# Causal attention with a channel mix on one core: seven block products for the last two batches' product with w_v, 1/sum applied to the exponentials of pairs 13 to 24, and a new order

## The chip, the cores and the metric

The kernel runs on one core of one Trainium2 chip. The time is device microseconds (us) of one execution; the kernel before takes 459.02 us, the median of three runs (458.9 to 459.26). The engines are TensorE (PE, matmuls; PEld is its weight load), VectorE (DVE), ScalarE (ACT), GpSimd (POOL) and SyncE (SP, which issues the DMAs).

## The reference: what is computed

There are 4 batches, 12 heads of width 64 and 448 positions. The attention's result, 768 wide, goes into a channel mix:

```
scores = scale * q @ k.T, masked above the diagonal
attn   = exp(scores - max) / (sum + 1e-9)
x      = attn @ v, heads side by side             (448 x 768 per batch)
xk     = mu_k * x + (1 - mu_k) * x_prev           (xr likewise with mu_r)
k      = relu(xk @ w_k)                           (768 -> 1024)
out    = sigmoid(xr @ w_r) * ((k * k) @ w_v)      (1024 -> 768)
```

## The kernel before, in words

Two heads make a pair; pairs are numbered 0 to 23 in the code (pair 13 of the title is `w` = 12), six to a batch. For a pair, `score` (L388, L401) makes the scores in three pieces `s_w_0`, `s_w_1`, `s_w_2` in a ring of two PSUM tiles; `row_max` and `row_top` (L418, L430, L432) find the row maxima, `exps` (L441) writes the exponentials `e` and their row sums `su`. `prob_hi` and `prob_lo` (L495, L499) split `e` in a high and a low float16 part `p`, `turn_p` (L505, issued by SP) transposes it by DMA into `pT`, a ring of three buffers for two per pair, and `weighted_all` (L563) multiplies by v: 36 matmuls into the one PSUM tile `bank`, called PV w below. These are divided by the row sums on the way out: `recip`, `recip_hi`, `recip_lo` (L455, L459, L466) make 1/sum, `turn_r` (one PE transpose, L472), `copy_r`, `spread` (four matmuls of 128x112, L482) and `spread_out` (L492) lay it out over the partitions, and `evac` (L580) multiplies `bank` by it. `mix_now`, `mix`, `mix_hi`, `mix_lo` (L228 to L234 as `scaled`, L607, L614, L618) make xk and xr. Pairs 0 to 5 take other ways for some of this.

The products with w_k, w_r and w_v are `step_mm` (L830): an output block of 128 columns by 448 positions is summed in one PSUM tile of a ring of two, with three matmuls of 128x448 per 128 rows of the weight (high x high, high x low, low x high). In a batch mk has 8 outputs of 6 steps (144 matmuls), mr 6 of 6 (108), mv 6 of 8 (144). `relu` and `square` take mk out, `k_scale`, `k_hi`, `k_lo` scale and split it, `r_copy` and `sigmoids` (L937) take mr, `y_mul` (L941) multiplies mv by the sigmoid and `y_out` (L947) stores 128x448.

What sets the order is a table of numbers, not the loops: every operation has a number in `CHOICE["starts"]`, and `Plan.run` issues all operations sorted by it, so each engine's queue is that order cut down to its engine. `CHOICE["engines"]` names the engine for operations that may run on several, `CHOICE["fills"]` where matmuls that only fill time stand. Within the table each engine waits by semaphores for the last reader or writer of the tile that it touches. Batch b's mr and mv stand among the attention of batch b + 1; for the last batch they stand alone at the end.

Of the kernel before, what the change touches and what calls it, by code (L numbers as in the profile page):

```python
# [33 lines left out]
class Plan:  # L34
# [57 lines left out]
    "plain": "kr",  # L92
    "short": "LLLLLLRRRRRRRRRRRRRRRRRR",
# [7 lines left out]
def tile_causal_attention_channel_mix(  # L101
# [98 lines left out]
    def x_of(w):  # L200
        return x_ts[w % NX]

    N8 = 2 * NCH
    diag = [const.tile([P, 2], F32, name=f"diag{i}") for i in range(2)]
    for t in diag:
        nc.gpsimd.memset(t, 0.0)
    spreads = []

    rs_t = []
    for i in range(2):  # L210
        t = const.tile([CP, P], F16, name=f"rs{i}")
# [223 lines left out]
    def exps(w, g, j, c):  # L435
        if w not in tot:
            tot[w] = p2.tile([CP, NCH, 2], F32, tag="su", name=f"su_{w}")
        if (w, j) not in em:
            em[w, j] = act.tile([CP, NB, CP], F32, tag="e", name=f"e_{w}_{j}", bufs=NE)
        o = STEPS[g][c]  # L440
        nc.scalar.activation(  # L441
            em[w, j][:, blocks(c)].rearrange("p a b -> p (a b)"),
            sps[w, g][:CP, j, o : o + CP * (c + 1)],
            AF.Exp,
            bias=stat[w][:, c, j : j + 1],
            scale=scale,
            accum_out=tot[w][:, c, j : j + 1],
        )
# [92 lines left out]
    def weighted(w, n):  # L541
# [19 lines left out]
        for i, (vi, pi) in enumerate(steps):  # L561
            for j in range(2):
# [18 lines left out]

    def plain(b, kind):

        return b == 0 and kind in CHOICE["plain"]

    def as_one(t):

        return t.rearrange("p a s -> p (a s)").bitcast(F32)

    def share(w, mu, part):  # L590
        m = w % NPAIR
        if plain(w // NPAIR, "kr"[mu]):
            return (shares_p if whole_p(w) else shares_h)[:, part, mu, m : m + 1]
# [219 lines left out]
    def step_mm(m, kind, o, i):  # L813

        b, t0, n = M[m]
        steps, w = {"k": (NO, wk), "r": (NO, wr), "v": (NF, late.get("W"))}[kind]
        if i == 0:
            mps[m, kind, o] = ps_m.tile([P, 512], F32, tag="m", name=f"m{kind}_{m}_{o}")
        ps = mps[m, kind, o][:, :n]
        x = kk[b, i] if kind == "v" else {"k": xk, "r": xr}[kind][b * NPAIR + i]  # L820
        cols = slice(o * P, (o + 1) * P)
        if kind not in CHOICE["plain"]:
            w = w[:, i]
        else:
            half = w.shape[-1]
            h, lo = divmod(o * P, half)
            w = final(i + NO * (kind == "r"), h)
            cols = slice(lo, lo + P)
        for a, (wi, xi) in enumerate(((0, 0), (0, 1), (1, 0))):
            nc.tensor.matmul(  # L830
                ps,
                w[:, wi, cols],
                x[:, xi, t0 : t0 + n],
                start=(i == 0 and a == 0),
                stop=(i == steps - 1 and a == 2),
            )
# [57 lines left out]
    def k_scaled(m, pk):  # L894
# [468 lines left out]
```

## Time and profile before

| | |
|---|---|
| median of three runs | 459.02 us |
| the profiled execution | 458.52 us |
| its span | 456.7 us |
| PE / DVE / ACT / POOL busy | 450.7 / 352.8 / 298.2 / 180.0 us |
| PE's share of the chain that ended last | 87% |

The span is what the trace covers; 1.8 us of the execution lie around it. Busy time is the sum of an engine's instructions. A matmul's own time in the trace is longer than its share of a row of matmuls, since they overlap: the step from one to the next is read from a row's whole time and its count.

### The profile page before, as it was taken

To read this page: it belongs to the slowest core of one execution; us is meant where nothing else is said; L and a number is where in the kernel's file an instruction comes from. 1 tells how busy PE (TensorE), PEld (TensorE's weight loads), DVE (VectorE), ACT (ScalarE), POOL (GpSimd) and SP (SyncE) were. 2 spreads that over 40 slices of the span, in tenths; PEclk is the share of its full clock that TensorE was granted. 3 is DMA by queue.
4 is the path that set the end of the run, shared out by engine and by line. 5 is a ranking of instruction groups with operands and counts; after the bars stand their busy time and mean duration, and the time that the engine had idled before them with its cause. 6 is when DMAs were issued, how large, how long until landed. Compare 5 with 4: busy or idle time off the path is not lost.

```text
span 456.7 us, 9334 instructions
## 1 busy us (share of the span) xinstructions
PE 450.7 (99%) x3525; PEld 260.3 (57%) x3525; DVE 352.8 (77%) x711; ACT 298.2 (65%) x815; POOL 180.0 (39%) x179
## 2 busy tenths in 40 slices
PE   8999999999999999999999999999999999999996
PEld 6566765545655566555556566555656565555553
DVE  6999999998898999898898878777888685243111
ACT  5999999999989957676769545576459322322400
POOL 5255752132403651412466863247553652104000
PEclk9999999999999999999999999999999999999999
DMA  8897754674077686364478763741744672000011
GB/s 309 292 356 278 262 199 176 235 165 93 2 161 162 123 175 158 72 152 90 93 142 142 155 150 101 157 118 40 136 80 81 121 123 82 0 1 0 22 41 60
DMA packets 94845, 60.57 MB, mean 133 GB/s; under 512 B 83408, under 2 KB 86480, under 8 KB 94032
## 3 DMA queue, kind: packets, MB, share of 16 engines
q1 hardware_dynamic: 94800, 59.98, 51.7%
q8 instruction: 27, 0.44, 0.4%
q14 instruction: 18, 0.15, 0.1%
HBM read 33.82 MB, written 5.51 MB: 86 GB/s over the span
## 4 chain that ended last, share of the span: by engine, by line
PE 87%; ACT 6%; DVE 5%; issue 1%; POOL 0%; ACTq 0%; DVEq 0%
PE mv L830 22%; PE mk L830 18%; PE mr L830 14%; PE mk L845 8%; PE s L401 8%; PE bank L563 7%; PE mr L845 4%; ACT e L441 3%; PE s L388 2%; DVE s L418 2%; PE eT L521 2%; PE sp L482 1%; PE bank L284 1%; DVE p L499 1%; ACT turned L531 1%
## 5 line engine op out<-in xcount | busy, mean ns | idle before, releaser
L830 PE MATMUL mv<-k,wv 128*128 128x448 f16 x576 | 113.1, 353 | 0.0
L441 ACT ACTIVATE e<-s,st 112x112 f32<-112x112 f32 (+3 forms) x192 | 93.1, 495 | 12.6 <-DVE st L432 7.8
L830 PEld LDWEIGHTS <-wv 128*128 128x128 f16 x576 | 54.9, 98 | 50.7 <-issue 1.8
L830 PE MATMUL mk<-xk,wk 128*128 128x448 f16 x432 | 83.4, 353 | 0.0
L418 DVE TENSOR_REDUCE s<-s 112x2 f32<-112x672 f32 (+3 forms) x96 | 70.7, 743 | 15.0 <-PE s L401 11.3
L830 PEld LDWEIGHTS <-wk 128*128 128x128 f16 x486 | 46.5, 98 | 43.8 <-issue 2.2
L830 PE MATMUL mr<-xr,wr 128*128 128x448 f16 x270 | 55.3, 352 | 0.0
L499 POOL TENSOR_TENSOR p<-e,p 112x1120 f16<-112x1120 f32 x15 | 36.5, 2435 | 40.2 <-ACT p L495 31.1
L830 PEld LDWEIGHTS <-wr 128*128 128x128 f16 x270 | 26.1, 99 | 23.3 <-issue 0.2
L441 ACT ACTIVATION_READ_ACCUMULATOR e<-s,st 112x1 f32 x192 | 39.3, 205 | 0.0
L941 DVE SCALAR_TENSOR_TENSOR a<-mv,kap,a 128x448 f32<-128x448 f32 x24 | 16.3, 679 | 29.6 <-PE mv L830 29.4
L845 PE MATMUL mk<-xk,wk 128*128 128x448 f32 x96 | 38.0, 546 | 0.0
L607 DVE SCALAR_TENSOR_TENSOR xf<-xt,shares,xf 128x448 f32<-128x448 f32 x36 | 29.4, 823 | 1.4 <-ACT xf L228 0.8
L845 PE MATMUL mr<-xr,wr 128*128 128x448 f32 x72 | 29.8, 550 | 0.0
L563 PEld LDWEIGHTS <-vs 112*64 112x64 f16 x648 | 26.8, 110 | 4.9 <-issue 4.1
L563 PE MATMUL bank<-pT,vs 112*64 112x224 f16 (+1 forms) x648 | 29.4, 245 | 0.0
L499 DVE TENSOR_TENSOR p<-e,p 112x1120 f16<-112x1120 f32 x21 | 28.2, 1341 | 1.4 <-ACT p L495 1.3
L845 PEld LDWEIGHTS mk<-xk,wk 128*128 128x128 f32 x96 | 17.6, 190 | 16.4 <-issue 15.6
L495 ACT CAST p<-e 112x1120 f16<-112x1120 f32 x22 | 24.7, 1122 | 3.4 <-DMA pT<-p 3.2
L430 ACT ACTIVATE st<-s 112x2 f32<-112x2 f32 (+1 forms) x34 | 5.8, 169 | 32.3 <-DVE s L418 32.1
L614 POOL CAST xr<-xf 128x448 f16<-128x448 f32 x12 | 11.1, 924 | 39.1 <-DVE xf L607 39.1
L401 PE MATMUL s<-ql,qh 64*112 64x112 f32 (+3 forms) x144 | 25.5, 351 | 0.0
(216 smaller groups left out, 829.2 us busy)
## 6 DMA issues: line engine op xcount, KB each, us to landing
qk<-in_qk_dram SPq DMA_DIRECT2D x24, 448.0 KB, 4.3
wraw<-in_w_k_dram SPq DMA_DIRECT2D x6, 1024.0 KB, 7.9
wraw<-in_w_v_dram SPq DMA_DIRECT2D x8, 768.0 KB, 4.7
vraw<-in_v_dram SPq DMA_DIRECT2D x24, 224.0 KB, 5.0
out_dram<-a SPq DMA_DIRECT2D x24, 224.0 KB, 2.5
wraw<-in_w_r_dram SPq DMA_DIRECT2D x6, 768.0 KB, 5.5
pT<-p SPq DMA_TRANSPOSE x36, 4.8
muT<-in_mu_dram SPq DMA_DIRECT2D x1, 6.0 KB, 4.3
```

The source lines that it names most:

```text
L388: nc.tensor.matmul(diagonal, pick[rows, h], fill, start=h == 1, stop=False, skip_group_check=True)
L401: nc.tensor.matmul(s[:CP, j, o : o + n], q_[rows, 0, c * CP : (c + 1) * CP], k_[rows, 1, :n], start=False, stop=c == max(STEPS[g]) and i = ...
L418: nc.vector.tensor_reduce(most(w, g, c, c + 1), s[:CP, :, o : o + CP * (c + 1)], AX.X, ALU.max, negate=True)
L441: nc.scalar.activation(em[w, j][:, blocks(c)].rearrange("p a b -> p (a b)"), sps[w, g][:CP, j, o : o + CP * (c + 1)], AF.Exp, bias=stat[w] ...
L495: copy[e](p_t[at_][:, :NB, :CP], em[w, j])
L499: tt[e](p[:, NB:, :CP], em.pop((w, j)), p[:, :NB, :CP], ALU.subtract)
L563: nc.tensor.matmul(px[w][64 * j : 64 * j + 64, cols], value(j, vi), p(j, pi), start=n == 0 and i == 0, stop=last and i == len(steps) - 1, ...
L607: nc.vector.scalar_tensor_tensor(f, x_of(w)[:, :S], share(w, mu, 1), f, ALU.mult, ALU.add)
L614: copy[e](dst[w][:, 0], xf[w, mu])
L830: nc.tensor.matmul(ps, w[:, wi, cols], x[:, xi, t0 : t0 + n], start=(i == 0 and a == 0), stop=(i == steps - 1 and a == 2),)
L845: nc.tensor.matmul(mps[m, kind, o][:, :n], z[:, o * P : (o + 1) * P], x, start=i == 0, stop=i == NO - 1)
L941: nc.vector.scalar_tensor_tensor(s, mps.pop((m, "v", o))[:, : M[m][2]], kap[m][:, 3:4], s, ALU.mult, ALU.mult)
```

## The change

`"sums"` marks pairs 12 to 23 with N. For these `divide` scales the eight blocks of `e` in place on ACT by 1/sum (four activations a head, 112 x 112, 224, 336 and 448), before `prob_hi`; `recip_hi`, `recip_lo`, `turn_r`, `copy_r`, `spread` and `spread_out` are dropped, and `evac_up` multiplies `bank` by a constant on ACT or DVE.

`"fast": "v"` takes the products of batches 2 and 3 with w_v together: k*k of the two batches and w_v are cut in two by two blocks, and seven block products stand for eight. Two of them are plain `step_mm` groups of batch 2, five are `fast_mm`. `s_sum`, `s_hi`, `s_lo` make sums of weight blocks and split them, `t_sum`, `t_hi`, `t_lo` sums of k*k blocks; `keep` and `fold` add up the products from PSUM, `y_fast` multiplies by the sigmoid. The five products of output block p are summed in the two halves (`side` 0 and 1) of one PSUM tile `fast_p`. The last output is stored in two halves of 224 positions. `first_blocks` leaves only outputs 0 and 1 of batch 2's mv, four steps each and then four more, among batch 3's attention; the rest stands at the end. The `starts` and `engines` tables are new but for their first part.

```diff
+    "sums": "------HHHHHHNNNNNNNNNNNN",
+    "fast": "v",
...
+    def divide(w, j, e):
+        for c in range(NCH):
+            x = em[w, j][:, blocks(c)]
+            scaled(x, x, tot[w][:, c, j : j + 1], e)
+
...
+    def evac_up(w, e):
+        x, p = x_of(w)[:, 1:], px.pop(w)[:, :S]
+        if e == "A":
+            nc.scalar.activation(x, p, AF.Copy, scale=UP)
+        else:
+            nc.vector.tensor_scalar(x, p, UP, None, ALU.mult)
...
+    def t_sum(i, k, e="D"):
...
+            nc.vector.scalar_tensor_tensor(x, x, r1, b11[:, 0], ALU.mult, ALU.subtract)
+        elif k == 1:
+            tt[e](x, x, b11[:, 1], ALU.subtract)
...
+    def s_sum(i, k, e):
...
+            tt[e](sf[i, 0], w_block("21", i)[:, 0], w_block("21", i)[:, 1], ALU.add)
...
+    def fast_mm(p, q, i):
+
+        w, x, side, begins = {
+            3: ("s4", "b", 0, False), 4: ("22", "4", 1, False), 5: ("s1", "1", 0, True),
+            6: ("s2", "2", 1, True), 7: ("s3", "3", 1, False),
+        }[q]
+        if p not in ps_b:
+            ps_b[p] = ps_s.tile([P, 2, 512], F32, tag="s", name=f"fast_{p}")
...
+        for a, (wi, xi) in enumerate(((0, 0), (0, 1), (1, 0))):
+            nc.tensor.matmul(
+                ps_b[p][:, side, :S],
...
+    def fold(p, k):
+        side, was, to = {2: (1, 1, None), 3: (1, 1, None), 21: (1, 1, 1), 12: (0, 2, 2)}[k]
...
+        nc.vector.tensor_tensor(part_sum[p, to], ps_b[p][:, side, :S], part_sum[p, was], ALU.add)
...
+        if not early_sums(w):
...
+            if early_sums(w):
+                plan.op(
+                    {"ACT": 1690}, 0, divide, (w, j),
+                    [(te, None, "w"), (tu, None, "r")],
+                )
...
+            mm(5)
+            plan.op(copied(n, True), 0, keep, (p, 5, 0), [(bk, "b", "r"), (*m5, "w")])
+            mm(6)
+            plan.op("DVE", dve(n), fold, (p, 2), [(bk, "c", "r"), *[(*x, "r") for x in m1_], (*u2, "w")])
+            mm(7)
...
```

**First place: PE between two pieces of the scores of pair 23, and ACT beside it.** On PE before, a row `rp_22` and 24 matmuls of mv stand behind the last piece of `s_23_0` (the scores `s_23_1` come after PV 21, seven microseconds later by the trace):

```order
L401 MATMUL s_23_0_4771<-qh_23_4641 112x224 x2
...
L388 MATMUL s_23_1_4887<-mask_97,pick_96 128x48
...
L388 MATMUL s_23_2_4900<-mask_97,pick_96 128x48 [waits Activation_49]
```

On PE now, `s_23_1` follows `s_23_0` at once, then come 12 matmuls of mv, and then `s_23_2`, which takes the PSUM tile of `s_23_0`:

```order
L404 MATMUL s_23_0_4747<-qh_23_4674 112x224 x2
...
L391 MATMUL s_23_1_4765<-mask_97,pick_96 128x48 [waits Activation_49]
...
L404 MATMUL s_23_1_4765<-qh_23_4674 112x336 x2
...
L391 MATMUL s_23_2_4809<-mask_97,pick_96 128x48 [waits Activation_49]
```

ACT's queue now, at the exponentials of `s_23_0`; the wait of `s_23_2` on ACT is for the fourth of them:

```order
L1138 ACT_TABLE_LOAD
L1138 ACTIVATE a_162<-a_162,krs_2_4029 128x448 x4
L1138 ACTIVATE a_162<-a_162,krs_2_4029 128x448 [waits Activation_49]
L1138 ACTIVATE a_162<-a_162,krs_2_4029 128x448 [waits DVE_49]
L444 ACT_TABLE_LOAD [waits DVE_49]
L444 ACTIVATE e_23_0_4794,su_23_4793<-s_23_0_4747,st_23_4776 112x112 [waits PE_49]
L444 ACTIVATE e_23_1_4797,su_23_4793<-s_23_0_4747,st_23_4776 112x112
L444 ACTIVATE e_23_0_4794,su_23_4793<-s_23_0_4747,st_23_4776 112x224
L444 ACTIVATE e_23_1_4797,su_23_4793<-s_23_0_4747,st_23_4776 112x224
```

The room between the first and the third piece of pair 23's scores went from mv of half a batch to `s_23_1` and 12 matmuls.

**Second place: PE from PV 22 to PV 23, and SP.** On PE before, 48 matmuls of mv, a `rp` and two `sp` stand between the last matmul of PV 22 and the first of PV 23:

```order
L563 MATMUL bank_148<-pT_22_1_4979,vs_22_4929 64x112
L830 LDWEIGHTS wv_1099
L830 MATMUL mv_2_4_5024<-k2_2_0_4318,wv_1099 128x448 [waits DVE_49]
...
L482 MATMUL sp_23_5114<-rt_23_5112,sel_119 128x112 [waits Activation_49]
...
L563 MATMUL bank_148<-pT_23_0_5053,vs_23_4951 64x224 [waits DVE_49]
L563 LDWEIGHTS vs_23_4951
L563 MATMUL bank_148<-pT_23_1_5058,vs_23_4951 64x224 [waits DMAHW5_49]
```

On PE now, six matmuls of mk stand there:

```order
L576 MATMUL bank_148<-pT_22_1_4874,vs_22_4900 64x112
L852 LDWEIGHTS wk0_1779
L852 MATMUL mk_3_1_4980<-xk_18_4467,wk0_1779 128x448 [waits DVE_49]
...
L852 MATMUL mk_3_0_4892<-xk_21_4973,wk_150 128x448 [waits Activation_49]
...
L852 MATMUL mk_3_0_4892<-xk_21_4973,wk_150 128x448 [waits Pool_49]
...
L576 MATMUL bank_148<-pT_23_0_4922,vs_23_4966 64x224 [waits DVE_49]
...
L576 MATMUL bank_148<-pT_23_1_4970,vs_23_4966 64x224 [waits DMAHW4_49]
```

SP's queue now; the wait of the last transpose on PE is for the last matmul of PV 22, which reads `pT_22_0`, the buffer that `pT_23_1` takes (ring of three):

```order
L518 DMA_TRANSPOSE pT_22_0_4788<-p0_140 128x20x112 [waits DMAHW6_49,PE_49,Pool_49]
L518 DMA_TRANSPOSE pT_22_1_4874<-p1_142 128x20x112 [waits DMAHW7_49,DVE_49,PE_49]
L518 DMA_TRANSPOSE pT_23_0_4922<-p0_140 128x20x112 [waits DMAHW0_49,DVE_49,PE_49]
L518 DMA_TRANSPOSE pT_23_1_4970<-p1_142 128x20x112 [waits DMAHW1_49,DVE_49,PE_49]
L1149 DMA out_0_dram<-a_162 128x448 [waits DMAHW5_49,DVE_49]
```

Before, the same ring held and the same wait stood in SP's queue, but with mv behind it on PE.

**Third place: PE and DVE in the last tile, `fast_2`.** On PE before, the program ends with mv in two tiles in turn and no wait within a group:

```order
L830 MATMUL mv_3_4_5651<-k2_3_6_5459,wv_1099 128x448
L830 LDWEIGHTS wv_1099
L830 MATMUL mv_3_4_5651<-k2_3_7_5550,wv_1099 128x448
```

On PE now, `fast_2` stands alone for 60 matmuls; three matmuls after a block product is complete, a matmul waits for the DVE instruction that reads it, whichever half of the tile it writes itself:

```order
L1085 MATMUL fast_2_5670<-wk_150,sw_5_5400 128x448
L1085 LDWEIGHTS sw_0_5186
L1085 MATMUL fast_2_5670<-wk_150,sw_0_5186 128x448
...
L1085 LDWEIGHTS sw_1_5192
L1085 MATMUL fast_2_5670<-wk_150,sw_1_5192 128x448 [waits DVE_49]
```

DVE's queue now beside it (a wait on PE is for the matmul right ahead of the waiting one):

```order
L1114 TENSOR_TENSOR p0_140<-fast_2_5670,xt0_92 128x448 [waits DVE_49,PE_49]
L1114 TENSOR_TENSOR p1_142<-fast_1_5496,p1_142 128x448
...
L1114 TENSOR_TENSOR u3_2_5714<-fast_2_5670,xt0_92 128x448 [waits PE_49]
...
L1107 COPY p0_140<-fast_2_5670 128x448 [waits PE_49]
...
L1114 TENSOR_TENSOR xt0_92<-fast_2_5670,xt0_92 128x448 [waits PE_49]
...
L1143 SCALAR_TENSOR_TENSOR a_162<-mv_2_2_5459,kap_2_4013,a_162 128x224 [waits PE_49] x2
```

From the last products of `fast_0` to the end of the program there are six such pairs of a read and a matmul that waits for it: five reads of 448 positions and one of 224.

## Rows read from the trace of the kernel before

**Rows 1.** The page: busy time, and PE's granted clock in 40 slices.
```profile
PE 450.7 (99%) x3525; PEld 260.3 (57%) x3525; DVE 352.8 (77%) x711; ACT 298.2 (65%) x815; POOL 180.0 (39%) x179
PEclk9999999999999999999999999999999999999999
```

**Rows 2.** Chain that ended last, 366 us to the end: start, us, what.
```profile
368.35 0.20 PE sp L482 x4
...
373.09 0.05 PE rp L472
...
425.85 27.25 PE mv L830 x144
453.11 0.03 issue
453.13 0.68 DVE a L941
```

**Rows 3.** PE's waits: for what, us in total, times, longest.
```profile
PE bank L280 <- DVE busy L148: 1.1, 1, 1.1
PE s L388 <- ACT e L441: 0.6, 3, 0.2
```

**Rows 4.** Groups by form: busy us, mean ns of one, idle before.
```profile
L830 PE MATMUL mv<-k,wv 128*128 128x448 f16 x576 | 113.1, 353 | 0.0
L580 DVE TENSOR_TENSOR xt<-bank,xt 128x448 f32<-128x448 f32 x24 | 14.9, 620 | 3.8 <-PE bank L563 3.4
L607 DVE SCALAR_TENSOR_TENSOR xf<-xt,shares,xf 128x448 f32<-128x448 f32 x36 | 29.4, 823 | 1.4 <-ACT xf L228 0.8
L618 DVE TENSOR_TENSOR xk<-xf,xk 128x448 f16<-128x448 f32 x11 | 6.8, 616 | 2.0 <-ACT xk L614 1.3 <-POOL xk L614 0.7
L441 ACT ACTIVATE e<-s,st 112x448 f32<-112x448 f32 x48 | 30.1, 633 | 2.8 <-DVE st L432 2.3
L441 ACT ACTIVATE e<-s,st 112x112 f32<-112x112 f32 x48 | 16.8, 355 | 6.1 <-DVE st L432 5.3 <-DVE rs L466 0.3
```

**Rows 5.** The transposed `pT`: SP's instructions, then issue to landing.
```profile
L505 SPq DMA_TRANSPOSE pT<-p x36: 2553/2734/4880, 90.3 to 369.1; - x36
...
DMA to landing us min/median/max: 4.5/4.8/7.3
```

**Rows 6.** Timeline of PE at pair 23: start, duration, what.
```profile
354.80 0.25 PE L388 MATMUL s<-mask,pick 64*128 64x48 bf16 x4
...
355.40 0.25 PE L388 MATMUL s<-mask,pick 64*128 64x48 bf16 x4
...
364.90 1.64 PE L563 MATMUL bank<-pT,vs 112*64 112x224 f16 x36
...
376.10 1.64 PE L563 MATMUL bank<-pT,vs 112*64 112x224 f16 x36
```

**Rows 7.** Timelines of DVE and ACT at pair 23's first scores.
```profile
348.55 1.06 DVE L418 TENSOR_REDUCE s<-s 112x2 f32<-112x224 f32 x2
...
349.71 0.17 ACT L430 ACTIVATE st<-s 112x4 f32<-112x4 f32 x1 [0.21 <-DVE s L418]
349.95 1.28 ACT L441 ACT_TABLE_LOAD   x1
351.25 0.35 ACT L441 ACTIVATE e<-s,st 112x112 f32<-112x112 f32 x1
...
351.60 0.44 ACT L441 ACTIVATE e<-s,st 112x224 f32<-112x224 f32 x1
```

**Rows 8.** Stretches: us, then busy us of PE, PEld, DVE, ACT, POOL; clock.
```profile
40.00:60.00 20.00, 19.78 (x211) 14.04 (x211) 19.04 (x35) 19.23 (x57) 11.89 (x13) 1.00 0.71 237
60.00:80.00 20.00, 20.00 (x99) 10.63 (x94) 18.92 (x40) 19.56 (x49) 7.15 (x6) 1.00 0.60 215
...
160.00:360.00 200.00, 199.99 (x1724) 116.86 (x1719) 168.55 (x305) 130.04 (x374) 98.71 (x85) 1.00 0.57 121
...
360.00:456.70 96.70, 93.09 (x556) 49.42 (x553) 38.10 (x72) 21.44 (x46) 16.65 (x18) 1.00 0.18 45
```

More of the change, by code (lines that the diff above doesn't have):

```diff
@@ L834, in step_mm @@
                 start=(i == 0 and a == 0),
-                stop=(i == steps - 1 and a == 2),
+                stop=(i == steps - 1 or (kind == "v" and fast(m) and i == HK - 1)) and a == 2,
+                skip_group_check=kind == "v" and fast(m),
             )
@@ L907, in k_hi @@
         b, t0, n = M[m]
+        if (b, f) not in kk and fast(m) and m == B - 1:
+            kk[b, f] = x_home("b", f - NF // 2)
         if (b, f) not in kk:
@@ new lines, in s_home @@
+    def s_home(q, i):
+        if q == "3":
+            return w_block("21", i)
+        n = 3 * i + "124".index(q)
+        if n // 2 not in sw:
+            if n < 8:
+                t = act.tile([P, NB, CP], F32, tag="e", name=f"sw_{n // 2}", bufs=NE).rearrange(
+                    "p a b -> p (a b)"
+                ).bitcast(F16)
+            else:
+                t = act.tile([P, 2 * NB, CP], F16, tag="pT", name=f"sw_{n // 2}", bufs=NPT).rearrange(
+                    "p a b -> p (a b)"
+                )
+            sw[n // 2] = t[:, : 4 * HW].rearrange("p (n t c) -> p n t c", n=2, t=2)
+        return sw[n // 2][:, n % 2]
@@ new lines, in p_home, with keep @@
+    def p_home(p, n):
+        if n == 2:
+            return p2.tile([P, S], F32, tag=f"xf{p % 2}", name=f"u3_{p}", bufs=1)
+        z = p_all[(p_at[p]) % 2].rearrange("p a b -> p (a b)").bitcast(F32)
+        return z[:, n * S : (n + 1) * S]
+    def keep(p, k, slot, e):
+        if k == 1:
+            part_sum[p, 1] = a_slot(slot, S)
+            src = mps[B - 2, "v", p]
+        else:
+            part_sum[p, 5] = p_home(p, 0)
+            src = ps_b[p][:, 0]
+        copy[e](part_sum[p, k], src[:, :S])
@@ L1168, in values, with step @@
         over_all(lambda: vmm[b], 1, CP, f"v{b}", lambda r: scaled_v(b, r), out_, 600 if also else 525, also)
-    def step(m, kind, o, i):
+    def step(m, kind, o, i, part=None):
         b, t0, n = M[m]
-        if i == 0:
+        if i == 0 and not (part and part[0]):
             order[m, kind, o] = ("m", nexts("m"), 2)
@@ new lines, in tile_causal_attention_channel_mix, with s_tile, s_sums, sum_ @@
+    s_tiles = {}
+    def s_tile(q, i):
+        if q == "3":
+            return (f"w{2 * NO + i}", 0, 1), "21"
+        n = 3 * i + "124".index(q)
+        if n // 2 not in s_tiles:
+            s_tiles[n // 2] = ("e", 2 * NW + n // 2, NE) if n < 8 else ("pT", 2 * NW + n // 2 - 4 + S_FIRST, NPT)
+        return s_tiles[n // 2], n % 2
+    S_FIRST = 2
+    def s_sums():
+        n = HW
+        for i in range(HK):
+            w1, w2 = (f"w{2 * NO + i}", 0, 1), (f"w{2 * NO + HK + i}", 0, 1)
+            if i % 2:
+                f = [(("xf0", NW + i // 2, 1), None), (("xf1", NW + i // 2, 1), None), (("x", NW + NX - 1, NX), None)]
+            else:
+                t = ("pT", 2 * NW + i // 2, NPT)
+                f = [(t, 0), (t, 1), (("vs", NW + i // 2, NVS), None)]
+            def sum_(k, reads, at_):
+                plan.op(less(n, True), 0, s_sum, (i, k), [(x, p, "r") for x, p in reads] + [(*f[at_], "w")], fast=True)
+            def split(q, at_):
+                t, part = s_tile(q, i)
+                hi, lo = (part, part) if q == "3" else ((part, "hi"), (part, "lo"))
+                src = [(*f[at_], "r")]
+                plan.op(copied(n), 0, s_hi, (q, i), src + [(t, hi, "w")], fast=True)
+                plan.op(less(n, True), 0, s_lo, (q, i), src + ([] if q == "3" else [(t, hi, "r")]) + [(t, lo, "w")], fast=True)
+            sum_(0, [(w1, "21")], 0)
+            sum_(1, [(w2, "22"), f[0]], 1)
+            sum_(2, [(w2, "22")], 1)
+            sum_(3, [(w1, "11")], 2)
+            sum_(4, [f[2]], 0)
+            split("1", 1)
+            split("3", 0)
+            sum_(5, [f[1]], 2)
+            split("2", 2)
+            sum_(6, [(w2, "12"), f[2]], 1)
+            sum_(7, [(w2, "12")], 1)
+            split("4", 1)
@@ new lines, in tile_causal_attention_channel_mix, with first_blocks @@
+    p_at = {}
+    m1_of = {}
+    def first_blocks(m):
+        n = S
+        for p in range(HO - 1):
+            for i in range(NF):
+                ps = step(m, "v", p, i)
+                if i == HK - 1:
+                    at_, m1_of[p] = a_next(n)
+                    plan.op(copied(n, True), 0, keep, (p, 1, at_), [(ps, None, "r")] + [(x, None, "w") for x in m1_of[p]])
+            s = s_of[m, p]
+            plan.op("DVE", dve(n, ap=True), y_mul, (m, p), [(ps, None, "r")] + [(x, None, "w") for x in s])
+            plan.op("SP", 475, y_out, (m, p), [(x, None, "r") for x in s], dma=717)
@@ L1236, in mix_v @@
         for o in range(NO):
+            if m == len(M) - 1 and o == NO - 1:
+                for part in ((0, n // 2), (n // 2, n // 2)):
+                    for i in range(NF):
+                        ps = step(m, "v", o, i, part)
+                    s = [s_of[m, o][part[0] // HALF]]
+                    plan.op("DVE", dve(n // 2, ap=True), y_mul, (m, o, part), [(ps, part[0], "r")] + [(x, None, "w") for x in s])
+                    plan.op("SP", 475, y_out, (m, o, part), [(x, None, "r") for x in s], dma=360)
+                continue
             for i in range(NF):
```

298 lines of the change are left out of this document (258 added, 40 removed).

## The prediction

> **What bounds the kernel now.** I read the page first. PE is busy for 450.7 of 456.7 us, DVE for 352.8, ACT for 298.2, and PE's granted clock is full in every slice [rows 1]. So PE is the bound if nothing makes it wait, which the view of waits answers: in the whole span PE waits 1.1 us once, at the start, and 0.6 us in three short pieces [rows 3]. The chain of waits agrees: its last 85 us are rows of matmuls without a gap, then 0.03 us and one DVE multiplication of 0.68 [rows 2]. Hence every matmul taken out of that chain is worth its step, and every wait put into it costs its length. A row of 144 matmuls of 128x448 lasts 27.25 us [rows 2], so a step is 0.189 us. A single such matmul takes 0.353 [rows 4]: its result is complete 0.353 - 0.189 = 0.16 us after the next could have started.
>
> **PE's saving.** The change takes 228 matmuls of 448 positions out of step_mm, and adds 24 of 224 there (worth 12) and 180 in fast_mm: 36 steps fewer, 36 x 0.189 = 6.8 us. For 12 pairs the four spread matmuls (0.20) and the transpose of 1/sum (0.05) go [rows 2]: 12 x 0.25 = 3.0 us. Together -9.8 us. The last multiplication now covers 224 positions instead of 448, and its store half as much: I take -0.3 us, between 0 and half of 0.68.
>
> **First place: the wait of s_23_2, +1.3 us.** s_23_2 needs the PSUM tile of s_23_0, so it waits until the fourth exponential of s_23_0 is done. Before, half a batch of mv lay between. Now PE has only s_23_1 and 12 matmuls there: 0.60 us (one score's start to the next [rows 6]) + 12 x 0.189 = 2.9 us. Meanwhile DVE and ACT need, from the same work in the trace [rows 7]: two reductions 1.06, the row constant 0.17, ACT's table load 1.28, which stands behind that constant in ACT's queue because sigmoids came before, then four exponentials: 0.35 and 0.44 twice, overlapping by 0.1, about 1.4. With 0.05 at each of five hand-overs this is 4.2. The wait is 4.2 - 2.9 = 1.3; 0.6 if the hand-overs vanish and the exponentials overlap more, 2.5 if ACT comes late to it.
>
> **Second place: PV 22 to PV 23, +3.8 us, and +0.4 behind it.** The last transpose takes the buffer that PV 22 reads, and SP starts it when PV 22 ends. Its data land 4.5 to 7.3 us after issue, 4.8 in the median [rows 5]. PE's second matmul of PV 23 needs them. Before, 9.6 us of matmuls lay between the two (from 366.5 to 376.1 [rows 6]), so the landing was hidden. Now there are six steps, 1.1 us. With 0.1 for SP's start: 4.8 + 0.1 - 1.1 = 3.8 us, bounds 3.5 and 6.3 by the ends of the row. What stands behind the waiting matmul on PE is all of PV 23, and behind that the scaled and mixed x of pair 23: five instructions (taking the bank out, two for the mix, high and low part) of 0.62, 0.62 and 0.82 [rows 4] and two that I put between 0.36 and 0.62, about 2.7 together, against 12 matmuls, 2.3: +0.4. The other early-summed pairs keep over 5 us of matmuls between one PV and the next in the order, more than the landing.
>
> **Third place: the last tiles, +5.2 us.** In fast_p a fold or keep on DVE reads one half; the next matmul in PE's queue waits for that read, though it writes the other half, and the read itself waits for the matmul right ahead of it. Nothing lies between, so PE stands for the last matmul's completion (0.16), two hand-overs (0.03 [rows 2], and as much again) and the read. Before has no such read; the nearest row is the DVE instruction that takes the bank out of PSUM, 0.62 [rows 4]. That makes 0.16 + 0.06 + 0.62 = 0.84. Five of these are 4.2 us; the one of 224 positions I take at 0.65; one more a little earlier has three matmuls as cover, 0.84 - 0.57 = 0.3. Together 5.2. Below: 0.6 each if the completion is counted twice, 3.7 in all. Above: with the 0.82 of the mix row, 6.4. That these waits stop PE is sure by the order; nothing else may pass them in PE's queue.
>
> **What lies beside other work, at zero.** The 96 divisions go to ACT. They are nearest to exponentials of the same widths, 0.355 to 0.633 us [rows 4], mean 0.49: 47 us. From 160 to 360 us ACT is busy for 130 of 200 us and DVE for 169 [rows 8]; ACT with the divisions is near 177 of some 195. That PE can run full beside so loaded engines is shown earlier: from 60 to 80 us with ACT 19.6 and DVE 18.9 of 20 PE loses nothing, from 40 to 60 with 19.2 and 19.0 it loses 0.22 [rows 8]. So I take 0 and keep 2.2 (0.22 per 20 us) as its bound. The new DVE work (26 weight sums, 25 sums of k*k, 27 low parts, 12 folds, 9 products y_fast, each near 0.62 [rows 4], some 55 us, less 6 us of y_mul and some 12 of evac and spread_out) falls mostly after 360 us, where DVE is busy for 38 of 97 us [rows 8]. That hides it, except at the reads of the third place. If the cover were gone, each late low part would cost PE its 0.62.
>
> **The sum**, against the profiled execution of 458.52 us: 458.5 - 9.8 - 0.3 + 1.3 + 3.8 + 0.4 + 5.2 = 459.1 us. The profiled execution lies 0.1% under the median of 459.02, within what separates the runs; I predict 459.1. About 0.2%, 0.9 us, is what a measurement of this kernel can tell from no change.
>
> **Rivals.**
> - *The waits are mostly covered (faster).* If the trace of before holds here too, where no PE wait after the start is longer than 0.2 us [rows 3], only the sure savings and half of the waits stay: 458.5 - 10.1 + 5.4 = 453.8 us. For it: that order kept PE full beside two loaded engines. Against it: at the two last places no instruction on PE lies between, so cover would have to come from shorter landings and reads than any row shows.
> - *ACT becomes the bound in pairs 13 to 20 (slower).* One division chain per head stands between the exponentials and the split, so the score after next waits for the tile and PV for the transpose. It decides once ACT's work from one pair's first score to the next exceeds PE's. ACT at 177 of 195 leaves 1.5 us a pair; a pair that exceeds it by 0.3 us, 12 times, costs 3.6: 462.7 us. Against it are the two stretches above.
> - *The clock falls at the second place (slower).* Before, the clock is full in all slices, but PE never pauses longer than 1.1 us [rows 1, 3], so no row shows what a pause near 4 us does. If PE's clock fell to the lower of its two levels, 1.2 GHz, a step would take 0.378 us; for a stretch as long as the pause itself, 3.8 us, that loses 1.9, for twice as long 3.8: 461.0 to 462.9 us. The Trainium skill, page "TensorE: Matmul & The Clock Gate", section "HAM oscillation — how this bites in real kernels", says that waits of some microseconds for a DMA between rows of matmuls send the clock to half; by that rule this is the result, and nothing in the trace of before bears on it.
>
> **How the numbers follow.** My forecast has a chance of 0.50, its own range 457.3 to 461.3 us by the bounds of the terms (the lower ends take 0.7, 0.3 and 1.5 off, the upper ends together add more, but not all at once). The covered waits have 0.22, ACT 0.13, the clock 0.10; 0.05 is for what I do not see. The range that leaves two in ten out is 454.5 to 462.5 us. Faster than 458.1: the covered waits, 0.15 of the forecast and 0.01 of the rest, 0.38. Within: 0.25 of the forecast and 0.01, 0.26. Slower than 459.9: 0.10 of the forecast, ACT, the clock and 0.03, 0.36.
>
> **What the profile of the changed kernel would show.** The view of waits would have new rows of PE: for the transposed p, one of 3.5 to 4 us in front of PV 23; for ACT's exponentials, one near 1.3 us in front of a score; for DVE's folds and keep, five or six of 0.6 to 0.7 in the last 20 us. PE's busy time would be some 10 us less, and its clock full throughout. A granted clock under 1.00 after PV 23 would speak for the clock; ACT as releaser of PE between 160 and 300 us, in many pieces, for the second rival; a last stretch without waits for the first. The forecast is wrong if PE's new waits add up to less than 8 or more than 13 us, or if they lie elsewhere than at the three places.

## The result: 465.29 us, slower by 1.4%

The changed kernel takes 465.29 us in the median of four runs (464.78 to 465.64), the kernel before 458.96 beside it: a ratio of 1.0137, 95% interval 1.0123 to 1.0151. The profiled execution takes 464.78 us, its span is 463.0. The forecast was 459.1 with a range of 454.5 to 462.5, so the change is slower and the time lies outside the range.

The page of the kernel after, busy time and PE's granted clock, against [rows 1]:

```profile
PE 446.0 (96%) x3441; PEld 256.7 (55%) x3441; DVE 391.0 (84%) x797; ACT 352.0 (76%) x923; POOL 167.5 (36%) x161
PEclk9999999999999999999999999999999799999999
```

PE's busy time fell by 4.7 us and its idle time (span less busy) grew from 6.0 to 17.0, by 11.0: together +6.3, the difference of the spans. One slice, at 360 us, has lost clock. Where the idle time is, the timeline of PE after shows (start, duration, engine, line, operation, count; in brackets the wait ahead of it and what ended it):

```profile
54.92 0.31 PE L391 MATMUL s<-mask,pick 64*128 64x96 bf16 x4 [0.78 <-ACT turned L544]
...
155.75 0.25 PE L391 MATMUL s<-mask,pick 64*128 64x48 bf16 x4 [1.41 <-ACT e L444]
...
350.04 0.25 PE L391 MATMUL s<-mask,pick 64*128 64x48 bf16 x4 [1.39 <-ACT e L444]
...
359.68 1.60 PE L576 MATMUL bank<-pT,vs 112*64 112x224 f16 x35 [0.52 <-DMA pT<-p]
363.74 2.02 PE L852 MATMUL mk<-xk,wk 128*128 128x448 f16 x6 [2.46 <-DVE a L1143]
...
366.58 2.96 PE L576 MATMUL bank<-pT,vs 112*64 112x224 f16 x35 [0.49 <-DMA pT<-p]
369.47 4.88 PE L852 MATMUL mk<-xk,wk 128*128 128x448 f16 x21
...
439.50 2.44 PE L1085 MATMUL fast<-xt,wv 128*128 128x448 f16 x12 [0.72 <-DVE p L1114]
...
445.50 0.73 PE L1085 MATMUL fast<-wk,sw 128*128 128x448 f16 x3 [0.71 <-DVE p L1114]
...
449.78 0.73 PE L1085 MATMUL fast<-wk,sw 128*128 128x448 f16 x3 [0.71 <-DVE u L1114]
...
451.79 1.86 PE L1085 MATMUL fast<-xt,wv 128*128 128x448 f16 x9 [0.71 <-DVE p L1107]
...
455.50 1.30 PE L1085 MATMUL fast<-wk,sw 128*128 128x448 f16 x6 [0.71 <-DVE xt L1114]
...
458.78 1.02 PE L852 MATMUL mv<-k,wv 128*128 128x224 f16 x9 [0.54 <-DVE a L1143]
```

Before had none of these [rows 3]. By place: two waits in the first 160 us, 2.2; the first place (s_23_2) 1.39; the second (PV 22 to PV 23) 0.52 + 2.46 + 0.49, and 0.17 at 374.51, 3.6; the last tiles 0.72 + 4 x 0.71 + 0.54, 4.1. That is 11.3, near the 11.0 of idle time that came.

At the second place the clock is the other half. Stretches of the kernel after (us, busy us of PE, PEld, DVE, ACT, POOL, PE's granted clock, DMA share, GB/s):

```profile
362.00:364.00 2.00, 0.26 (x2) 0.16 (x2) 2.00 (x4) 1.13 (x2) 0.89 (x1) 1.00 0.56 103
364.00:366.00 2.00, 2.00 (x7) 0.56 (x6) 2.00 (x6) 0.67 (x1) 0.15 (x1) 0.54 1.12 214
366.00:368.00 2.00, 1.51 (x21) 1.42 (x21) 1.40 (x4) 0.00 (x0) 0.00 (x0) 0.50 0.62 222
...
370.00:372.00 2.00, 2.00 (x10) 0.90 (x8) 1.74 (x4) 0.58 (x2) 0.00 (x0) 0.75 0.01 4
```

After the wait of 2.46 us PE runs at 0.50, the lower of its two levels (1.2 GHz), until about 371 us. The Trainium skill, page "TensorE: Matmul & The Clock Gate", section "HAM oscillation — how this bites in real kernels", says that waits of some microseconds for a DMA between short rows of matmuls send the clock to half. The trace agrees on the half clock, with the 0.50 above; but the longest wait here is 2.46 us, for an instruction of DVE, while the page's case has longer ones.

### The profile page after: what moved, and what is told of

Its sections match the earlier page's. It is cut to its first block, busy times and chain, and to the rows that moved or that the text cites. A ratio compares the mean times of both kernels' runs of the same rounds, so it can differ in the third digit from the quotient of the medians.

```text
span 463.0 us, 9335 instructions
## 1 busy us (share of the span) xinstructions
PE 446.0 (96%) x3441; PEld 256.7 (55%) x3441; DVE 391.0 (84%) x797; ACT 352.0 (76%) x923; POOL 167.5 (36%) x161
## 4 chain that ended last, share of the span: by engine, by line
PE 76%; DVE 11%; ACT 6%; DMA 4%; issue 2%; POOL 1%; ACTq 0%; DVEq 0%; SPq 0%
PE mk L852 17%; PE mr L852 13%; PE mv L852 10%; PE mk L868 8%; PE fast L1085 7%; PE s L404 7%; PE bank L576 6%; PE mr L868 3%; DVE s L421 3%; ACT e L444 3%; DMA pT<-p 2%; PE s L391 2%; DMA wraw<-in_w_r_dram 2%; DVE p L512 1%; DVE wk L762 1%
## 5 line engine op out<-in xcount | busy, mean ns | idle before, releaser
L444 ACT ACTIVATE e<-s,st 112x336 f32<-112x336 f32 (+3 forms) x192 | 92.8, 492 | 13.2 <-DVE st L435 7.2
L852 PE MATMUL mv<-k,wv 128*128 128x448 f16 (+1 forms) x372 | 71.9, 347 | 0.6 <-DVE a L1143 0.5
L512 POOL TENSOR_TENSOR p<-e,p 112x1120 f16<-112x1120 f32 x17 | 40.5, 2383 | 44.5 <-DVE p L508 22.3
L852 PEld LDWEIGHTS <-wv 128*128 128x128 f16 x372 | 35.1, 98 | 32.5 <-issue 3.4
L231 ACT ACTIVATE e<-e,su 112x112 f32<-112x112 f32 (+1 forms) x96 | 42.2, 516 | 2.7 <-DVE su L463 2.7
L627 DVE SCALAR_TENSOR_TENSOR xf<-xt,shares,xf 128x448 f32<-128x448 f32 x36 | 26.5, 739 | 1.8 <-ACT xf L231 1.3
L512 DVE TENSOR_TENSOR p<-e,p 112x1120 f16<-112x1120 f32 x19 | 25.2, 1328 | 1.3 <-ACT p L508 1.1
L728 POOL TENSOR_SCALAR wraw<-wraw 128x768 int32<-128x768 uint16 (+1 forms) x17 | 19.4, 1142 | 17.0 <-DMA wraw<-in_w_v_dram 9.1
L1085 PE MATMUL fast<-wk,sw 128*128 128x448 f16 x108 | 21.9, 352 | 2.3 <-DVE p L1114 0.7
L391 PE MATMUL s<-mask,pick 64*128 64x48 bf16 (+3 forms) x288 | 19.7, 213 | 4.4 <-ACT e L444 3.3
```

What stands on the lines that cost most here:

```text
L231: nc.scalar.activation(dst, src, AF.Copy, scale=s)
L391: nc.tensor.matmul(diagonal, pick[rows, h], fill, start=h == 1, stop=False, skip_group_check=True)
L444: nc.scalar.activation(em[w, j][:, blocks(c)].rearrange("p a b -> p (a b)"), sps[w, g][:CP, j, o : o + CP * (c + 1)], AF.Exp, bias=stat[w] ...
L627: nc.vector.scalar_tensor_tensor(f, x_of(w)[:, :S], share(w, mu, 1), f, ALU.mult, ALU.add)
L728: nc.gpsimd.tensor_scalar(t, u, TOP3, -0.499, ALU.mult, ALU.add)
L852: nc.tensor.matmul(ps, w[:, wi, cols], x[:, xi, t0 : t0 + n], start=(i == 0 and a == 0), stop=(i == steps - 1 or (kind == "v" and fast(m) ...
```

## What holds PE up at the second place

The chain of waits of the kernel after from PV 21 to the work behind PV 23 (start, us, what):

```profile
353.44 6.20 DMA pT<-p
...
359.73 0.76 DVE p L508
...
360.51 1.34 DVE p L512
...
361.91 4.63 DMA pT<-p
...
366.58 2.96 PE bank L576 x32
```

Two landings stand in a row, not one. Pair 23's second split (L508, L512) writes the p buffer that the transpose of pair 22 still reads. It begins when that has landed, 6.20 us after its issue, and only then can the last transpose go, 4.63 more. Behind the split in DVE's queue stands y_mul (L1143), which frees the PSUM tile that the six matmuls of mk take: that is PE's 2.46. So the end of this place is set by landing, split, landing; how the wait divides among PE's instructions matters little. How much the first landing adds can be read too. DVE's timeline has a wait of 0.90 us for it ahead of the split, but the last transpose also waits for the last matmul of PV 22, which ends at 361.28 (359.68 + 1.60), and it went at 361.91. Without the first landing it could have gone some 0.6 us earlier at most, an estimate from these rows.

## The experiments

Diffs leave out the table of numbers and the places of the fills, which are renumbered. Each run of a kernel was compared with the kernel before on the same chip.

**Keep PE busy around PV 23 (e1_fill).**

```diff
+    def warm(w, n):
+        t = ps_t.tile([P, 512], F32, tag="t", name=f"warm_{w}")
+        for i in range(n):
+            nc.tensor.matmul(t[:, :P], busy, busy, start=i == 0, stop=i == n - 1, skip_group_check=True)
...
+        if w == NW - 1:
+            warm(w, 28)
         for n in range(len(PV)):
             weighted(w, n)
+        if w == NW - 2:
+            warm(w, 40)
```

> 68 matmuls of 128x128 without use, into the small PSUM tile that nobody reads, keep PE busy in the two long waits between PV 22 and PV 23 (40 right behind PV 22, 28 right ahead of PV 23); nothing else is moved. After has PE's clock at 0.50 to 0.54 from 364 to 370 us. Theory: the clock falls because PE stands still there; with the filler it stays at 1.00, the waits keep their ends, and the time falls by what the low clock cost: six mk matmuls 0.9, PV 23 1.4, 21 mk matmuls 0.9, together 3.2 us, less up to 0.5 that the filler is longer than the waits: 462.1 to 462.6 us. Rival: the rows are slow there for another reason (transfers that run beside them); then the clock column stays low and the time is 465.3 to 465.8.

Measured: 464.02 us (463.15 to 465.54), ratio to before 1.0095 [1.0062, 1.0128]. PE's timeline:

```profile
360.33 1.60 PE L576 MATMUL bank<-pT,vs 112*64 112x224 f16 x35 [0.52 <-DMA pT<-p]
361.87 2.41 PE L588 MATMUL warm<-busy 128*128 128x128 f16 x40
364.39 1.29 PE L861 MATMUL mk<-xk,wk 128*128 128x448 f16 x6
...
367.18 1.68 PE L576 MATMUL bank<-pT,vs 112*64 112x224 f16 x36
...
371.79 1.67 PE L861 MATMUL mk<-xk,wk 128*128 128x448 f16 x8 [0.31 <-DVE xk L647]
```

The clock stays at 1.00, PV 23 takes 1.68 instead of 2.96, the six matmuls of mk 1.29 instead of 2.02. Yet from PV 22's wait to the row of mk that follows km (374.51 after, 373.63 here) it is 13.30 us instead of 14.83: 1.5 gained. The six matmuls lay inside the landing's wait anyway, and an x that the slow clock had hidden is now waited for, 0.31. By the profiles the clock costs 1.5 net, half of the 3.2 expected; its gross price is worked out further down, with PE's saving. The medians differ by 1.3, and the intervals of the two ratios overlap (1.0062 to 1.0128 here, 1.0123 to 1.0151 after); e10_three shows the gain clear of the noise.

**Half 0 of fast_2 in a tile of its own (e2_bank).**

```diff
+        to = bank if p == HO - 1 and side == 0 else ps_b[p][:, side]
...
-                ps_b[p][:, side, :S],
+                to[:, :S],
...
-        nc.vector.tensor_tensor(part_sum[p, to], ps_b[p][:, side, :S], part_sum[p, was], ALU.add)
+        src = bank if p == HO - 1 and side == 0 else ps_b[p][:, side]
+        nc.vector.tensor_tensor(part_sum[p, to], src[:, :S], part_sum[p, was], ALU.add)
```

> Half 0 of the last tile fast_2 is put into the PSUM tile bank, which is free by then; the same matmuls and DVE instructions in the same order. Theory: PE's waits in the tail stand between halves of one tile that share no data; with two tiles four of the waits of 0.71 us (0.85 with the last matmul's completion) go, and two reads keep three matmuls as cover (0.28 each): 465.3 - 3.4 + 0.6 = 462.5 us. Rival: DVE, with folds and y_fast, sets the pace of the tail; then the waits move to the next fold and the time stays within 0.5 us of 465.3.

Measured: 460.18 us (458.54 to 461.86), ratio 1.0018 [0.9999, 1.0038]. PE's timeline at PV 23 and in the last tile:

```profile
366.71 1.94 PE L576 MATMUL bank<-pT,vs 112*64 112x224 f16 x35 [0.16 <-DMA pT<-p]
...
449.77 2.43 PE L1086 MATMUL bank<-wk,sw 128*128 128x448 f16 x12
452.04 1.60 PE L852 MATMUL mv<-k,wv 128*128 128x224 f16 x15
454.18 1.02 PE L852 MATMUL mv<-k,wv 128*128 128x224 f16 x9 [0.54 <-DVE a L1145]
```

The four waits of 0.71 are gone. From the row of mk that follows km to PE's last matmul it is 81.8 us (373.42 to 455.20) instead of 85.3 (374.51 to 459.80): 3.5 us, which is 4 x (0.71 + 0.16), so the completion of the last matmul is lost with each wait, as the forecast had it; the 0.28 expected to stay at each of two reads did not. The rest of the 5.1 is mostly the second place, where in this profile PV 23 took 1.94 us and not 2.96, since the clock came back sooner. That differs between executions of this kernel: the six with a granted clock of 0.996 in the mean of the span take 458.54 to 460.21 us, the four with 0.992 or 0.993 take 460.65 to 461.86. All four of the changed kernel have 0.993. At like clock the tile is worth its 3.5 and little more: 465.3 less the 461.5 that those four take in the median is 3.8.

**y_mul ahead of the split (e3_ymul):** `y_mul(2,1)` moved in DVE's queue before `prob_hi(23,1)`.

> Only y_mul of batch 2's output 1 is moved, on DVE, from behind the split of pair 23's second head to ahead of it, so that the PSUM tile for mk's output 1 is free when PV 22 ends; the wait of 2.46 us on PE that the trace puts down to it goes. Theory A (landing): the last transpose's landing ends the stretch, and PE now waits in front of PV 23 for the 2.5 us longer: 465.3, within 0.6 us. Theory B (DVE's queue): the 2.46 us were the cost, and the time falls to 462.8.

Measured: 465.9 us (465.18 to 467.45), ratio 1.0137 [1.0104, 1.0169]. PE's timeline:

```profile
365.34 0.35 PE L852 MATMUL mk<-xk,wk 128*128 128x448 f16 x1 [1.12 <-ACT xk L634]
366.45 0.54 PE L852 MATMUL mk<-xk,wk 128*128 128x448 f16 x2 [0.77 <-POOL xk L638]
...
368.78 2.96 PE L576 MATMUL bank<-pT,vs 112*64 112x224 f16 x35 [1.57 <-DMA pT<-p]
```
```profile
368.00:370.00 2.00, 1.22 (x17) 1.22 (x18) 1.53 (x5) 0.00 (x0) 0.00 (x0) 0.50 0.70 243
```

The wait for y_mul is gone and 1.12 + 0.77 + 1.57 = 3.46 stand in place of 2.46 + 0.49 = 2.95: the landing sets the end, whichever matmul waits. The second fence is the stretch in which PV 23 begins, its clock behind the five busy times: it fell here too (0.50), though no wait is longer than 1.57 us. This profile is of the longest of the four executions, 467.45 us with a mean clock of 0.989; the others, at 0.993, take 465.18 to 465.91, as the changed kernel does.

**The order of before up to pair 9's scores (e4_first).** Only the table of numbers changes. The cut lies near 122 us by the trace, not at 185 as I had put it.

> The operations up to the first score of pair 9 (some 185 us) stand in the order of the kernel before; everything from there on is that of the changed kernel. Theory: the new order of the first part brought PE's waits of 0.78 us (at 54.9) and 1.41 us (at 155.8); they go, and since PE is the bound from there on, nothing later gives the time back: 465.3 - 2.2 = 463.1 us, without these two rows of waits. Rival: a later chain (sigmoids, exponentials, transposes at pair 23) sets the end whatever happened before it, or the first part's waits come from the new operations and not its order: 465.3, within 0.5 us.

Measured: 465.28 us (464.48 to 468.48), ratio 1.0132 [1.0088, 1.0176]. The wait at 55 us is gone, that at 155 us stays, 1.42, since the cut is ahead of it. PE's rows from PV 23 on, in the profiled execution of 464.48 us:

```profile
365.83 2.96 PE L576 MATMUL bank<-pT,vs 112*64 112x224 f16 x35 [1.31 <-DMA pT<-p]
368.72 5.30 PE L852 MATMUL mk<-xk,wk 128*128 128x448 f16 x21
374.19 4.13 PE L852 MATMUL mk<-xk,wk 128*128 128x448 f16 x21 [0.17 <-DVE km L911]
```

The landing moved with PE: PV 23's second matmul starts 0.75 us earlier than after (366.58), and its wait is longer mainly because the six matmuls of mk ran at full clock (1.29 us instead of 2.02). The slow clock takes back over half of it: it ends near 371 us in both profiles, so the row of 21 mk lasts 5.30 instead of 4.88, the row behind km starts 0.32 us earlier and the span is 0.3 shorter. The median did not change, against the expectation.

**The same up to pair 12's scores (e8_first).**

> The changed kernel, with the order of before up to the first score of pair 12, so that both waits that the new order brings in the first 160 us (0.78 at 55 us, 1.41 at 156 us) should go. Theory (these waits are an addition of their own): 465.3 - 2.2 = 463.1 us. Rival (what PE gains early is given back at PV 23, where it waits for a transposed p whose time is set by DVE, ACT and SP): the waits in front of PV 23 grow by as much, and the time stays at 465.3.

Measured: 478.0 us (473.72 to 478.84), ratio 1.0395 [1.0347, 1.0444]. It tells nothing of the first part: the seam between the two orders brings worse waits of its own. Rows of DVE, then the one of PE that waits for it:

```profile
152.33 1.33 DVE L512 TENSOR_TENSOR p<-e,p 112x1120 f16<-112x1120 f32 x1 [4.97 <-ACT p L508]
...
154.56 0.62 DVE L593 TENSOR_TENSOR xt<-bank,xt 128x448 f32<-128x448 f32 x1
```
```profile
155.23 3.01 PE L576 MATMUL bank<-pT,vs 112*64 112x224 f16 x36 [5.50 <-DVE xt L593]
```

DVE's instruction that takes out the bank stands behind a low half whose high half ACT makes late, behind a batch's sigmoids. Inconclusive.

**The table load in ACT's idle time (e5_exp).**

```diff
             nc.scalar.activation(sg[m, o], sg[m, o], AF.Sigmoid, scale=krs[m])
+        if m < B - 1:
+            nc.scalar.activation(first_in, first_in, AF.Exp)
```

> The changed kernel with one exponential of a single element on ACT right behind the sigmoids of batches 0 to 2, so that ACT's table load (1.28 us) stands in its idle time before the first row maxima and not between the row constant and the exponentials. Theory (the load is on the path to s_23_2 and s_10_2): the wait at s_23_2 goes from 1.39 to about 0.5 us, that at s_10_2 from 1.41 to about 0.4, and the chain to PV 23 comes 0.8 earlier: the time falls by 1.7 to 2.6 us, to 462.7 to 463.6. Rival (the exponentials' wait is for the reductions, and the load is beside them): both waits stay and the time stays at 465.3.

Measured: 462.02 us (461.76 to 462.82), ratio 1.0064 [1.0047, 1.0081]. Rows of PE, then of ACT:

```profile
154.37 0.25 PE L391 MATMUL s<-mask,pick 64*128 64x48 bf16 x4 [0.41 <-ACT e L444]
347.93 0.25 PE L391 MATMUL s<-mask,pick 64*128 64x48 bf16 x4 [0.65 <-ACT e L444]
```
```profile
344.86 1.28 ACT L1140 ACT_TABLE_LOAD   x1
346.15 0.20 ACT L1140 ACTIVATE firstin<-firstin 128x1 f32<-128x1 f32 x1
```

The load now lies between the sigmoids and the row constants; the wait at s_10_2 fell from 1.41 to 0.41, that at s_23_2 from 1.39 to 0.65. The medians differ by 3.3 us, the two profiled executions by 2.0; the two waits explain 1.7. The profiled execution has the mean clock of the kernel after, 0.993, and the other three have 0.996, so 2.0 is the gain at like clock.

**Only the divisions, in the order of before (e6_sums).** `"sums"` with N for pairs 12 to 23; the rest as before, each division right ahead of the split of its head.

> The kernel before, in its own order, with only the part on 1/sum: the 96 divisions of pairs 13 to 24 on ACT, and without the spread matmuls, the transposes of 1/sum and the copies of its spread; eight block products and their order as before. Theory (ACT's divisions cost nothing, as the sum had it): PE's 12 x 0.25 = 3.0 us come off whole, 459.0 - 3.0 = 456.0 us. Rival (ACT's chain of divisions delays the split and the scores, 0.3 us a pair or more): the gain is used up, 459 us or more, with ACT as the releaser of PE in many pieces.

Measured: 496.42 us (495.58 to 497.86), ratio 1.0818 [1.0794, 1.0843]: both numbers missed by far. PE waits 11.5 us for exponentials, 7.1 for DVE's kmm, 4.2 for a. Its longest wait, and ACT's queue ahead of it:

```profile
204.60 0.32 PE L389 MATMUL s<-mask,pick 64*128 64x48 bf16 x4 [5.62 <-ACT e L442]
```
```profile
198.58 0.35 ACT L442 ACTIVATE e<-s,st 112x112 f32<-112x112 f32 x1
...
200.41 1.78 ACT L229 ACTIVATE e<-e,su 112x112 f32<-112x112 f32 x4
202.22 1.12 ACT L506 CAST p<-e 112x1120 f16<-112x1120 f32 x1
203.25 0.44 ACT L442 ACTIVATE e<-s,st 112x224 f32<-112x224 f32 x1
```

Between the first and the second exponential that s waits for stand 4.2 us of other work, 1.78 of it divisions of the pair before. ACT is busy for 16.6 of the 20 us from 200 to 220: it is the place in the queue, not the load, that stops PE. This shows what an order made without the divisions does with them, not what they cost where the order was made for them.

**A quarter of the divisions (e11_quarter).** It leaves 72 of the 96 divisions out, so those blocks of e stay undivided.

```diff
         for c in range(NCH):
             x = em[w, j][:, blocks(c)]
-            scaled(x, x, tot[w][:, c, j : j + 1], e)
+            if c == 0:
+                scaled(x, x, tot[w][:, c, j : j + 1], e)
```

> The changed kernel with only the first of the four divisions of each head (24 of 96; the other blocks of e stay undivided, so part of the result is left out), in the same order. ACT loses 72 instructions, some 37 us. Theory (ACT's divisions lie beside PE's work, as the sum had it): 465.3 us, within 0.9. Rival (they set when the split, the transposes and the scores come, above all at pair 10 and at PV 23): 462 us or less, and the waits at 156 us and in front of PV 23 shorter.

Measured: 465.12 us (464.48 to 465.77), ratio 1.0129 [1.0114, 1.0145]. The stretch from 160 to 360 us, of the kernel after and then of this run:

```profile
160.00:360.00 200.00, 198.04 (x1698) 114.72 (x1698) 168.25 (x316) 174.27 (x468) 79.80 (x62) 1.00 0.57 123
```
```profile
160.00:360.00 200.00, 198.04 (x1695) 114.63 (x1695) 169.20 (x316) 142.56 (x397) 81.17 (x62) 1.00 0.57 124
```

ACT loses 31.7 us in this stretch and PE's busy time stays the same to the last digit; the waits at 156 and 350 us stay 1.41 and 1.39. In the new order these 72 divisions cost nothing; the 24 that stay were not taken out.

**Two repairs, and three (e9_two, e10_three):** e5's load and e2's tile; then e1's useless matmuls as well.

> The changed kernel with two repairs that each helped alone: the early table load (by a one-element exponential behind the sigmoids) and half 0 of fast_2 in the tile bank. Theory (the two lie apart in time, so their gains add): 465.3 - 3.3 - 5.1 = 456.9 us, under the kernel before. Rival (of the 5.1 only the tail's 3.5 is the tile's, the rest was a run in which PV 23 happened to wait less): 465.3 - 3.3 - 3.5 = 458.5 us, no different from before.

> The same two repairs and, as a third, the 68 useless matmuls of 128x128 that keep PE busy around PV 23. Theory (the clock's fall there is a loss of its own): 1.5 us under the run with two repairs, 455.4 to 457.0, and the granted clock full throughout. Rival (with the earlier exponentials the pause is short enough, or the useless matmuls delay PV 23 by as much as the clock gives back): the same as with two.

Measured: 460.12 us (458.11 to 460.94) with two, ratio 1.0019 [1.0006, 1.0031]; 458.23 (457.4 to 460.82) with three, ratio 0.9985 [0.9971, 0.9998]. Rows of PE with two; then PEclk of the page with three:

```profile
362.15 1.29 PE L852 MATMUL mk<-xk,wk 128*128 128x448 f16 x6 [2.45 <-DVE a L1147]
365.00 2.96 PE L576 MATMUL bank<-pT,vs 112*64 112x224 f16 x35 [1.34 <-DMA pT<-p]
373.63 20.59 PE L852 MATMUL mk<-xk,wk 128*128 128x448 f16 x108 [0.16 <-DVE km L911]
```
```profile
PEclk9999999999999999999999999999999999999999
```

By the medians the gains of e5 and e2 do not add: with both the time is that of e2 alone. The clock is why. PV 23's second matmul starts at 365.00 us here and at 366.71 in e2's profile, so the 1.7 of the earlier load arrive there. Then PV 23 runs at half clock in full (2.96 us, 1.94 in e2's profile), and from the next mk to the row of mk behind km it is 5.74 us against 4.84; from PV 22's wait to that row it is 15.54 us (358.09 to 373.63) against 13.58. Over all executions, ten of the eleven here have a mean clock of 0.991 to 0.993, but only four of e2's ten. With the clock kept up that stretch is 13.28 us, and by the medians the third repair is worth 1.9. Taken at like clock the gains nearly add: 465.3 - 3.5 for the tile - 2.0 for the load is 459.8 us, for 460.2 in the median of those ten executions, and less 1.5 for the clock it is 458.3, for 458.23. This version is the fastest of all, 0.7 us under the kernel before, by an interval that barely leaves 1.

**All repairs with a reworked second place (e7_all):** e5's load and e2's tile, the order of e8_first, PV 20 and PV 22 earlier, and mk steps ahead of PV 23.

> The changed kernel with all repairs together: the early order of before, the early table load, half 0 of fast_2 in the tile bank, and around PV 23 the PVs of batch 3 earlier and the mk steps ahead of PV 23 in place of behind it. Theory (three kinds of waits and the clock make up the loss): 465.3 - 2.2 (early) - 0.9 (first place) - 3.6 to -5.1 (second place, the clock stays full) - 3.5 (tail) = 453.6 to 455.1 us. Rival (one wait takes the place of another, as in the run with y_mul earlier): the tail's 3.5 alone stays, 461 to 462 us.

Measured: 478.24 us (477.44 to 478.96), ratio 1.0419 [1.0401, 1.0437]. It carries e8_first's seam (7.0 us in front of a PV, 3.6 at mv), so its total says nothing of the other repairs; at the second place it waits 2.22 + 0.78 + 1.63 + 0.31 = 4.9 us against 3.6, so that rework is no gain either.

## Why the prediction was wrong, point by point

- **PE's saving, 9.8 us: as forecast, within half a us, by this working.** PE's busy time fell by 4.7. The slow clock adds 2.8: the six matmuls of mk 2.02 - 1.29, PV 23 2.96 - 1.68, and the row of 21 mk 4.88 against the 4.13 that such a row takes at full clock (20 x 0.189 + 0.353 [rows 2, 4]). The thirteen waits listed add some 0.16 each, 2.1. 9.8 - 2.8 - 2.1 is 4.9, for 4.7 measured. e10_three, at full clock, agrees: PE is busy for 445.7 us, 4.1 of it useless matmuls, so 441.6, which is 9.1 under before with the completions of its waits still in it.
- **First place, 1.3: right, 1.39.** The table load on its path was right too; e5_exp takes it off, and 0.65 is left.
- **Second place, 3.8 + 0.4: the size near (3.6 of waits), the mechanism half right.** Of the 3.6, 2.95 lie between PV 22 and PV 23 and 0.17 behind; 0.52 lie ahead of PV 22's second matmul, where none was forecast. The landing sets the end, but PE's longest wait is y_mul behind the split, which itself waits for the landing of the transpose before. I followed SP's queue and not DVE's, which came out near because the split ended only 0.6 us behind PV 22. The 2.7 us of five instructions behind PV 23 add up to 2.8 to 3.3 by the durations given there, so the 0.4 should have been 0.5 to 1.0; at full clock (e1_fill) 0.31 + 0.17 of waits are there. e3_ymul shows that the sum does not hang on y_mul.
- **Third place, 5.2: right.** 4.1 of waits and 0.16 for each of six is 5.1; the price of one is 0.71 + 0.16, not 0.84, and e2_bank takes four of them away for 3.5. The one with three matmuls as cover, put at 0.3, shows no wait, so the sum came out right in part by luck.
- **ACT's divisions at zero: right**, by e11_quarter, for 72 of the 96; ACT's busy time from 160 to 360 us came out at 174, for 177. The rival that ACT bounds pairs 13 to 20 has fallen for this order. In the order of before the divisions do stop PE (e6_sums), but by their place in ACT's queue and not by ACT's load, which was the rival's condition.
- **The step that failed is the sum: it had no term for the clock.** "PE's busy time would be some 10 us less, and its clock full throughout" was the forecast, and the fall a rival with 0.10, at 1.9 to 3.8 us. It fell, for about 7 us after a wait of 2.46, at a gross price of 2.8 and, by e1_fill and e10_three, 1.5 to 1.9 net: the rest of the 2.8 lies where PE would wait for the landing or for x at full clock. Having forecast a pause of 4 us in a row of matmuls, with no row that showed the clock to outlast one, I should have put it into the sum.
- **The second fault: the sum had no term for what moved in the first 160 us.** The forecast said that waits would lie at the three places; 2.2 us lie elsewhere. The larger is the first place's mechanism again, at s_10_2. ACT's row there, after and then before:

```profile
150.27 1.28 ACT L444 ACT_TABLE_LOAD   x1
```
```profile
144.67 1.28 ACT L441 ACT_TABLE_LOAD   x1
```

  Before, the load begins 5.6 us earlier and the score waits for nothing. I worked the mechanism out for pair 23 and did not look for the other batch ends where the new order has it.

Forecast and measurement then differ by 464.8 - 459.1 = 5.7 us in the profiled execution: 2.8 for the clock, 2.2 + 0.3 for the early waits with their completions, and 0.4 that I can't place. This is where PE's time went, not what each cause is worth: with the clock held up only 1.5 to 1.9 comes back. Of the early waits, e5_exp takes 1.0 of the 1.41 away and the gain stays. The 0.78 at 55 us is settled only so far: with it gone PV 23 came 0.75 earlier, and over half of that went to the slow clock (e4_first). What the first part as a whole costs is open, since e8_first tells nothing of it. A third buffer of p, which would break the chain of two landings, was not tried; by the rows above it could bring some 0.6 us at most.

## What to carry to other kernels

Where a change takes work off the engine that bounds a kernel, ask what that work had covered: here 9.8 us of matmuls went and 11 us of waits appeared, in which landings, reads and a table load that had been hidden set the end. A pause of PE is priced at its length and at the slow matmuls behind it, and a mechanism found at one place is to be looked for at every place with the same pattern. A gain ahead of a stretch at half clock can be lost in it, as PE then does more of its work there (e4_first, e9_two). So a repair is judged between executions with the same mean clock, or with the clock held up; done so, the three repairs here nearly add up.

## What the runs showed of the hardware

- Short pauses in a row lowered the clock. In the kernel after 0.52 and 2.46 us of waits, with 1.6 us of PV between them, were followed by 0.50 for some 7 us; in e3_ymul waits of 0.55, 1.12, 0.77 and 1.57, none longer, were too. The single pauses of 1.39 and 1.41 us were not (PEclk is 9 in their slices). Useless 128x128 matmuls kept it at 1.00 in the profiles of e1_fill and e10_three.
- How long it stayed low differed between executions: some 7 us in the profile after, 3.4 in e2_bank's (0.50 from 364 to 366 us, 0.64 from 366 to 368). It shows in the mean clock (0.993 and 0.996) and in the time.
- An ACT table load takes 1.28 us wherever it stands (all eight in each of the profiles of before, after and e5_exp), and a one-element exponential behind the sigmoids (0.20 us) moves it into idle time.
- 32 us less of ACT's work in 200 us changed nothing (e11_quarter); some of the same work at a worse place in the same queue went with 37 us more (e6_sums).
